# First eight score tiles read keys where they were loaded, token tiles 2 and 3 transposed by DMA, and a new order table

## The chip, the cores and the metric

The kernel runs on one core of a Trainium2 chip. The metric is the device time of one execution in microseconds (us), as the median of several runs. Engines are named as the profile names them: PE (TensorE matmul), PEld (TensorE weight load), DVE (VectorE), ACT (ScalarE), POOL (GpSimd), SP (SyncE, which issues all transfers here).

## What is computed

Attention over 4 batches, 8 heads, 768 positions, head size 64, in which each query sees the keys less than 16 positions away and, of every block of 32 keys, one summary (the maximum of the keys, the mean of the values). Its output, laid out as 3072 tokens of 512, goes through a layer norm and a two-layer network with a residual:

```python
k_sum = k.reshape(B, H, nb, block, D).max(axis=3)
v_sum = v.reshape(B, H, nb, block, D).mean(axis=3)
scores_l = scale * np.matmul(q, k.transpose(0, 1, 3, 2))      # kept where |i - j| < 16
scores_s = scale * np.einsum('bhsd,bhnd->bhsn', q, k_sum) + np.log(block)
a = softmax(concatenate([masked scores_l, scores_s]))
x = np.matmul(a, concatenate([v, v_sum]))                      # heads side by side: tokens x 512
xn = (x - mu) / np.sqrt(var + 1e-06) * g_ln
out = x + np.maximum(xn @ w_ch1, 0.0) @ w_ch2                  # 512 -> 2048 -> 512
```

Attention inputs are float32; the two weight matrices arrive as float64.

## The kernel before

**Tiles.** There are 24 token tiles T of 128 tokens and 48 score tiles t = 2T + hh, each for four heads. Batch 0 is score tiles 0 to 11 (`NEARLY`), which go the early way, in float32: `early_k`, `early_qk`, `softmax`, `early_transp`, `early_pv`. The others go by 16-bit pairs (`load_q`, `load_k`, `qk`, `transp`, `pv`). Two score tiles make a token tile; `ln` norms it and `lnT` transposes it into the 16-bit pair `xs`, two token tiles to a pair g. `lnT` does this on PE for T below `PET` (four 128x128 transposes into `tx`, then a copy on ACT and a subtraction on DVE), and for later tiles by a copy and a subtraction into `x16` and one DMA transpose of it.

**Keys of batch 0.** `fetch_k0` loads the keys of each head pair hp into the tile `k0[hp]`, the two heads of a pair on the two halves of the partitions (0 to 63, 64 to 127). `batch_k(0, hp)` takes the block maxima into `ksum` (printed `kmax`). `early_k` then copies, for one score tile, its window of keys and the 24 maxima side by side into `kx`: two copies on ACT, three on POOL. `early_qk` makes four float32 matmuls of 184 or 192 columns out of it, two variants v by the two halves pr.

**Network.** `fetch_w` loads 512 KB of float64 weights, `dec_w` takes them apart on DVE with a square on ACT for the scale, `conv_w` makes 16-bit pairs `wp` (high on ACT, low on DVE). `g1` makes hidden tiles `h` (12 matmuls to a half), `g2` the sums `a`. Later pairs use a Strassen scheme (`sp1`, `sp2`, `sw2`).

**Order.** Every step is recorded, not issued. `ORDER` gives the order in which steps are recorded, which sets who gets a tile's buffer first; `BANKS` gives each PSUM tile its bank; `RANKS` gives each instruction a priority. `Plan.schedule` is a list scheduler with costs for every operation: on each engine it takes the ready instruction with the lowest rank, and `Plan.issue` writes the instructions in the order of these planned starts. Each engine runs its own list in order. Where the plan has a gap on PE in the first tiles, `issue` repeats the `spare` transpose as a filler.

Of the kernel before, what the change touches and what calls it, by code (L numbers as in the profile page):

```python
# [39 lines left out]
PET = 4  # L40
# [20 lines left out]
    "&=&D&E%e%s%v%w%x&$&%%y%z&'%{&&%}&#%|&(&*&)&+$Y&.&/&>&X&`&]&V&W&Y&b&f&a&c&k&l&t&C&d&e&g&Z&[&^&_&h&z&m&n&o&p&r'<"
    "&u&v&q&w&x&y&{'>&?&@&B&J&R&H&P&N&L&F&G&I&K&M'E&s'B'='?'G'@'P'F'H'I'R&|'K'Y'Q'S(#(,()(%(-(2($('(+&}'A'C'D'V'T'U"
    "(('[&T'u'Z']'w(&'J'L'^(3'W'X'{'_(6(*(0&O&Q&S&U'v'x'y'z'|(8&i&j'#':'2'6','.'8'0'4'M'N'O'`(7(9(/(B(C'a'b(<'c(:(;"
    "(=(A(D(L'}(>(G(P(E(F(H'-'/'1'3(J(K(M(N(O(Q(.'5'7'9';(I(R(S'd'i'k'm's'q'g'e'f'h'o'j'l'n'p'r't(?(@'$'%'&'''(')'*"
    "'+(T(Z(1(4(5(_(U(](^(`(a(b(d(q(f(g(h(V(c(e(w(i(j(k(s(m(W(l(r(t(|(u(v(x(y)4(n)%(o(p(z({(})#)$)&)')()))0)/).)1)9"
    ")2)3)7)8):);)<)>)D)C(X(Y([)B)E)5)6)H)F)G)I)J)a)=)?)@)Q)A)M)K)L)N)O)])P)R)S)})Z)w)[)^)y)_)`)x)z){)|)*)+),)-*()b"
    ")c*-*'*)***2*+*,*.*/)T)U)V)W)X)Y*1*#*$*6*%*&)d)j)m)h)n)p)s)o)t)l)f)r)q)u*=*<)k)g)e*0*3*4*5*7*8*9*:)i)v*G*;*H*F"
    "*I*J*Z*Q*P*L*O*R*]*S*T*V*K*M*N*a*d*U*W*j*[*^*_*`*b*c*y*f*e*g*h*i*k*s*u*|*@*A*t*v+#*w*x*z*{*}+$+.+%+&*>*?+,*X*Y"
    "*B*C*l+'*m*n*D*E+-+/+0+1+3+D+6+5*o*p+7+8+F+(+9+:+)+;+<+M+2+4+=+>+S*q*r+E+G+O+H+I+K+N+P+Q+R+T+b+Y+*+++?+@+J+L+U"
    "+V+W+h+_+X+Z+[+]+^+`+a+A+B+C+c+d+e+f+g+i+j+k+l+m+n+o+p"  # L70
)
BANKS = (
    "12530273542251030314674216774060434256124251601472762136360451327560463215645471030640110237575136624013707045"
    "32146345212504317031760552660743271231726517467633246515277642500121313460310361345270764326502055016666372467"
    "1073547435543201211012061232150306721475261765430136455052417156033547751464572670105161023450"
)
RANKS = (
    "#X#F#&#>$@#0#$#2#6#'#:#?#W#4#8#%#(#*#/#,#+#C#Y#L#V#S#=#R#Z#B#^#[%p#3#k$7$<#{$,#<#j#A$-$1$4$9$=#g&=%N#.#P##$}%,"
    "#9%:%h%l%d#x$Y$N#y#}$+$2#1#7#;#@#I#D#K#E#)#M#Q$5#J$;$?$E$I#5#`#d#N#a#f#O#T#]#h#q#l#v#s#t#w#z#|$%$.$#$)#p#o#m#r"
    "#n#c$K$X$b$j#U$W$c$k$x%&%*%0%5%?%>%7%<%8%;%@%L%Z%^#G#e#i#H#_#b#u$'$>$0$B$D%E%P$8$3$:$6$A%O%Y%e%r%y%|&+$&$*$$$/"  # L80
    "$($H$Q$U$d$`$]$i$f$r%c%i$s%g%o%v&'&/&8#-$F%%%-%D%s'2';'d%4%m'i(0&6'F'K't$C$G$L$T$a$h$l$n$t$z$u%'%/%R%a$p$J%6%="
    "%C%K$y%[%f%}&)$M$m%9%B%H$o$q$w${%F&&%`%{&*&9&D&H&K$Z$^$[$g$_&E&Q&S&[&`&c&f%1$P$S$O$V$R%J%S%V%]%_%n%k&$%x&5&?&M"
    "%t%W%u%T%U&@&P&^&k'$'@'B'D'>$e%A%I%M%b$v$|%+%2%j%q%w%z&%&-(N&C'=&e'3&3&|%)%3%.&#&>&B&I&L&Z&i&u&J&N&U&Y&r&x&{'G"
    "'L'V'S'X'W'R&,'q&1&.%$&4&w'C'N%G'I'Q'`'n&(&0&7&;&F&V&b&l&m'''0&G&X&]&j&o&y&}&a&d&s&v'#'+'('/'H'O'^'c'a'['f'r'u"
    "'v'|(*(.(6&_&R&W&O&T&g'%')'.'1'4':'P(%&q(5&n&p','-'7'<'A'J'T'_'e'j'l'm'h's'{(#('(-(1(9(?%#%('g'p'}(F(L(Y(d(}'6"
    "'E(&(a(y)8)J)M'Z'k($(+&<&h&t&z(,(J(R(W(T(f(p(O(M([(Z(m(s&A(3(<(D(G'8'5'w()(/(;&:'9)))2)9)='z(4(B(S'Y(=(I(X(E(q"
    ")():(8(P'M'U'o'x(V(](`(c(((j(r(v({)*)$).)A)a),)4)/)6)b)T)5)@)>)I)<)C(x)')3)G*')O*-)m*;+1)|*^'y(H(K(U(t)?(|)#)%"
    ")&'?(_(e)K)N)7)U)Z)d)g)q)^)w)h*5*Q*B*V)F*H*N*S*X*Z*Y*[)-)_)f)j)l)e){*$*)*.(b(l(i(g(n(o)Q)n)V)p)S)W)Y)[*c*g*`*w"
    "+F+I,%,+,4,1,.,C)L)r)u)z)}'*(^(w)0)E);)i)k)o)s*%*(*+*/*3*7,7*9*=*<*?*A*F*>*C*e*l*z*}*r+?+J+^(Q(k(u)B)])`(z)P)R"
    ")c*0*2)1)x*#*&***@*I*O*R*T*],;*_*d*b*h*j*o*n*q+,+9+@+x*y+3+;+o)H*1*8*k*t)X)t)v)D*,*4*a*p*D+)+6+:+=+N+X+b,&*L*W"  # L90
    "*f+H(>(7(@(2(:+'+-+0+2+5+L+P+O+W+V+]+g+l+},),@,I,V,T,X,W*6*J*P+a+|,$,',*,-,3,8,F,M,S,0,=*K*{+&+++/*m+8+<+C+G,J"
    "*i+A+D+K+S+i+t,#,]*s+d+k+w+z,Y,h,w,{--,}-$-8->-B-G-K-],6,Q,^,z)y*:*E*U*x+$+#+%+*+.+4+j+Y+_+T*v+R+Z+`+e,(,,,2,5"
# [1547 lines left out]
```

## Time and profile before

| what | value |
|---|---|
| median of 3 runs | 602.65 us (601.69 to 604.08) |
| the profiled execution | 602.32 us, its span 600.5 us |
| PE busy | 585.4 us (97% of the span) |
| DVE busy | 527.8 us (88%) |
| ACT busy | 425.4 us (71%) |
| POOL busy | 195.5 us (33%) |
| granted TensorE clock, mean | 0.999 |

The span is the time from the first to the last instruction of the profiled execution; 1.8 us of that execution's time lie around it. Busy time of PE includes the fillers and the warm-up transposes. "Idle" below is the span or stretch less the busy time of that engine.

### The profile page before, as it was taken

To read this page: it belongs to the slowest core of one execution; us is meant where nothing else is said; L and a number is where in the kernel's file an instruction comes from. 1 tells how busy PE (TensorE), PEld (TensorE's weight loads), DVE (VectorE), ACT (ScalarE), POOL (GpSimd) and SP (SyncE) were. 2 spreads that over 40 slices of the span, in tenths; PEclk is the share of its full clock that TensorE was granted. 3 is DMA by queue.
4 is the path that set the end of the run, shared out by engine and by line. 5 is a ranking of instruction groups with operands and counts; after the bars stand their busy time and mean duration, and the time that the engine had idled before them with its cause. 6 is when DMAs were issued, how large, how long until landed. Compare 5 with 4: busy or idle time off the path is not lost. (4 is left out here: it accounts for less than half of the span.)

```text
span 600.5 us, 16320 instructions
## 1 busy us (share of the span) xinstructions
PE 585.4 (97%) x6055; PEld 444.0 (74%) x6055; DVE 527.8 (88%) x1351; ACT 425.4 (71%) x968; POOL 195.5 (33%) x355
## 2 busy tenths in 40 slices
PE   7989999999999999999999989999999999999997
PEld 6579846864975885786686776777687886987876
DVE  5999999999899999989979978799999989678465
ACT  4899967798886889478968586577688655473241
POOL 5121400044557554724333323226444310230000
PEclk9999999999999999999999999999999999999999
DMA  8995485528968968677986894657456653412300
GB/s 312 340 332 171 148 259 159 178 66 224 234 161 206 227 183 180 159 170 193 213 206 125 186 197 116 126 156 174 101 128 149 101 155 70 102 29 46 80 2 35
DMA packets 138175, 96.07 MB, mean 160 GB/s; under 512 B 96112, under 2 KB 120944, under 8 KB 138096
## 3 DMA queue, kind: packets, MB, share of 16 engines
q1 hardware_dynamic: 138096, 95.04, 62.9%
q8 instruction: 47, 0.77, 0.6%
q14 instruction: 32, 0.26, 0.1%
HBM read 66.27 MB, written 6.29 MB: 121 GB/s over the span
## 5 line engine op out<-in xcount | busy, mean ns | idle before, releaser
L563 PE MATMUL a<-wp,hh 128*128 128x512 f16 x640 | 190.4, 379 | 0.0
L563 PEld LDWEIGHTS <-wp 128*128 128x128 f16 x1968 | 152.3, 98 | 17.5 <-DMA xs<-x 0.8
L563 PE MATMUL a<-wp,hl 128*128 128x512 f16 x320 | 121.3, 379 | 0.0
L563 PEld LDWEIGHTS <-hh 128*128 128x128 f16 x736 | 68.8, 98 | 58.6
L563 PE MATMUL h<-xs,wp 128*128 128x256 f16 x960 | 109.5, 273 | 0.8 <-DMA xs<-x 0.7
L563 POOL TENSOR_TENSOR p<-p,p 128x512 f16<-128x512 f32 x72 | 74.0, 1039 | 101.8 <-ACT p L563 65.3
L563 ACT ACTIVATE p<-p,mn 128x184 f32<-128x184 f32 (+1 forms) x192 | 76.3, 441 | 12.2 <-DVE mn L563 11.9
L563 PEld LDWEIGHTS <-wd 128*128 128x128 f16 x1176 | 70.5, 98 | 9.8 <-issue 3.6
L563 PEld LDWEIGHTS <-hl 128*128 128x128 f16 x368 | 36.0, 98 | 38.9 <-DVE hl L563 0.6
L563 DVE CUSTOM_DVE_ANT_0 p<-s,mask,sv 128x184 f32<-128x184 f32 x144 | 52.8, 398 | 2.2 <-PE s L563 2.0
L563 ACT ACTIVATE in<-in 128x384 f32<-128x384 f32 (+2 forms) x66 | 39.2, 595 | 16.5 <-DVE kmax L563 5.4
L563 POOL COPY ksg<-ksum 128x48 f32<-128x48 f32 x48 | 20.9, 439 | 78.3 <-DMA ksg<-in_kt 62.9
L563 PE MATMUL qx<-xs,wp 128*128 128x128 f16 x672 | 43.4, 219 | 0.0
L563 ACT CAST p<-p 128x512 f16<-128x512 f32 x72 | 33.9, 507 | 1.0 <-DMA pT<-p 0.5
L563 DVE SCALAR_TENSOR_TENSOR x<-a,wsc,x 128x512 f32<-128x512 f32 x40 | 29.5, 740 | 2.7 <-PE a L563 2.6
L563 ACT ACTIVATE v<-vst,sv 128x512 f16<-128x512 f32 x36 | 25.8, 719 | 7.7 <-PE o L563 7.6
L563 ACT ACTIVATE xn<-x,mv,rs 128x512 f32<-128x512 f32 x20 | 16.3, 814 | 18.6 <-POOL mv L563 15.6
L563 ACT ACTIVATE hh<-h 128x512 f16<-128x512 f32 x40 | 23.9, 602 | 5.6 <-PE h L563 5.3
L563 DVE SCALAR_TENSOR_TENSOR qhl<-qs,sv,qhl 64x512 f16<-64x512 f32 x36 | 27.5, 765 | 0.1
L563 PEld LDWEIGHTS <-pT 128*128 128x128 f16 x720 | 25.6, 98 | 2.5
L563 DVE SCALAR_TENSOR_TENSOR v<-vst,sv,v 128x512 f16<-128x512 f32 x36 | 26.8, 745 | 0.7 <-ACT v L563 0.7
L563 PE MATMUL o<-v,pT 128*128 128x65 f16 (+1 forms) x720 | 27.2, 193 | 0.0
(257 smaller groups left out, 1277.7 us busy)
## 6 DMA issues: line engine op xcount, KB each, us to landing
raw<-in_w SPq DMA_DIRECT2D x32, 512.0 KB, 6.8
qs<-in_qt SPq DMA_DIRECT2D x72, 128.0 KB, 2.9
ksg<-in_kt SPq DMA_DIRECT2D x48, 184.0 KB, 2.9
out_x<-x SPq DMA_DIRECT2D x20, 256.0 KB, 2.9
in<-in_ks SPq DMA_DIRECT2D x24, 192.0 KB, 3.0
...
```

What stands on the lines that cost most here:

```text
L563: getattr(getattr(nc, self.ops[i].engine), op)(*a, **k)
```

## The change

`PET` goes from 4 to 2 and `DK = 8` is new. For the score tiles 0 to 7 `early_k` is not called, and `early_qk` reads the keys from `k0` and the maxima from `ksum` by separate matmuls into the same columns of the PSUM tile: two for v = 0 (160 and 24 columns), three for v = 1 (128, 32 and 32), where there was one each. `ksum` of batch 0 gets 32 columns for each head pair, cleared first, so that the third piece fills its columns. Score tiles 8 to 11 keep `kx`. Token tiles 2 and 3 take the `x16` way with a DMA transpose. The three tables are new throughout.

```diff
-PET = 4
+PET = 2
+DK = 8
...
 ORDER = (
-    "#)$Z#7#%$i#+#k#5#6#3#4$[#1#8$k#,$g$h#'$^###W#(#l#0#/#2#D$l#$$b$]$m#&#9#;#:#E#F#G#H#K#I#X$_$v#*#=#>#?#@#A#B#C#J"
+    "$b$T#+#&#9#($`#%#h#3#U$R#/#;$W#4###1#2#g$U$a#7$X#,#*#0$V#'#:#E$Z#=#>#?$]#$#F#G#H#J#@$S#5#6#A#B#C#)#<$8#8$e$c$d"
...
@@ batch_k
-            bt["m", b] = work("kmax" if b else "ksum", f"kmax{b}", [P, 4, NB], F32, 1 + (b == 0))
+            bt["m", b] = work("kmax" if b else "ksum", f"kmax{b}", [P, 4, NB if b else BLK], F32, 1 + (b == 0))
+            if b == 0:
+                nc.gpsimd.memset(bt["m", b][:], 0.0)
...
@@ early_qk
-                    q, k = qw[T][r].rearrange("p (h v l) -> p h v l", h=2, v=2)[:, hh], kx[t % 2][r]
-                    nc.tensor.matmul(ps[pr][:, v * NE : v * NE + w], q[:, v], k[:, v, :w], start=True, stop=True)
+                    q = qw[T][r].rearrange("p (h v l) -> p h v l", h=2, v=2)[:, hh]
+                    parts = [(0, kx[t % 2][r, v, :w])]
+                    if t < DK:
+                        s, m = k0[2 * hh + v][r, P * T : P * T + P + BLK], bt["m", 0][r, 2 * hh + v]
+                        parts = [(D, s[:, :P]), (0, s[:, P:]), (BLK, m)] if v else [(0, s), (P + BLK, m[:, :NB])]
+                    for at, k in parts:
+                        at += v * NE
+                        nc.tensor.matmul(ps[pr][:, at : at + k.shape[1]], q[:, v], k, start=True, stop=True)
...
@@ attend
         if t < NEARLY:
-            early_k(t)
+            if t >= DK:
+                early_k(t)
             early_qk(t)
```

What the new tables do to the order, at three places.

**The first score tile on PE.** Names ahead of the arrow are PSUM tiles (`s_0`, `s_1` the two halves pr); `kx`, `k_0`, `k_1`, `kmax` are the keys, `qw` the queries. Before:

```order
L563 MATMUL s_0_121<-kx,qw_94 128x184
L563 MATMUL s_1_122<-kx,qw_94 128x184
L563 MATMUL s_0_121<-kx,qw_94 128x192
L563 MATMUL s_1_122<-kx,qw_94 128x192
L563 MATMUL spare<-ident 128x128
```

Now:

```order
L563 MATMUL s_0_119<-k_0_90,qw_94 128x160
L563 MATMUL s_0_119<-kmax_109,qw_94 128x24
L563 MATMUL s_1_120<-k_0_90,qw_94 128x160
L563 MATMUL s_1_120<-kmax_109,qw_94 128x24
L563 MATMUL s_0_119<-k_1_91,qw_94 128x128
L563 MATMUL s_0_119<-k_1_91,qw_94 128x32
L563 MATMUL s_0_119<-kmax_109,qw_94 128x32
L563 MATMUL s_1_120<-k_1_91,qw_94 128x128
L563 MATMUL s_1_120<-k_1_91,qw_94 128x32
L563 MATMUL s_1_120<-kmax_109,qw_94 128x32
```

Four matmuls that alternated between the halves are ten, of which two or three in a row are on the same half.

**PE in front of the first hidden tile `h`.** `pp` are transposes of probabilities, `o` attention outputs, `tx` token-tile transposes. Before:

```order
L563 MATMUL o_229<-tail,pT_0_226 128x2x65
L563 MATMUL o_229<-vw_101,pT_0_226 128x65 x2
L563 MATMUL o_229<-tail,pT_1_228 128x2x65
L563 MATMUL o_229<-vw_101,pT_1_228 128x65 x2
L563 MATMUL pp_0_240<-ident,p_89 128x128 x3
L563 LDWEIGHTS wp_165
L563 MATMUL h_257<-xs_219,wp_165 128x256
```

Now:

```order
L563 MATMUL pp_0_247<-ident,p_89 128x128 x3
L563 MATMUL pp_1_245<-ident,p_89 128x128 x3
L563 MATMUL o_249<-vst_77,pT_0_248 128x2x65
L563 MATMUL o_249<-vw_101,pT_0_248 128x65 x2
L563 MATMUL o_249<-vst_77,pT_1_246 128x2x65
L563 MATMUL o_249<-vw_101,pT_1_246 128x65 x2
L563 LDWEIGHTS wp_207
L563 MATMUL h_278<-xs_229,wp_207 128x256
```

The last `pp` and the last output tile of the first eight score tiles stand ahead of the first `h` now; before they came between the first `h` matmuls.

**SP at its start and around the new DMA transposes.** `k` are the keys, `raw` the weights. At the start, before:

```order
L563 DMA k_3_93<-in_ks 128x768
L563 DMA k_1_91<-in_ks 128x768
L563 DMA qw_94<-in_qe 128x512
L563 DMA k_0_90<-in_ks 128x768
L563 DMA k_2_92<-in_ks 128x768
```

Now, and further on the two transposes of token tiles 2 and 3 (`in_` are loads of batch 1 for its scales):

```order
L563 DMA k_0_90<-in_ks 128x768
L563 DMA k_1_91<-in_ks 128x768
L563 DMA qw_94<-in_qe 128x512
L563 DMA k_2_92<-in_ks 128x768
L563 DMA raw_111<-in_w 128x1024
L563 DMA k_3_93<-in_ks 128x768
...
L563 DMA in_2_281<-in_ks 128x384
L563 DMA_TRANSPOSE xs_243<-x_2_244 128x8x128
L563 DMA in_3_282<-in_ks 128x384
L563 DMA_TRANSPOSE xs_243<-x_3_255 128x8x128
```

The fourth load of keys stands behind 512 KB of weights, and the second transpose behind a load that needs a staging buffer.

## Rows read from the trace of the kernel before

**Rows 1.** Page, part 1: busy us of PE (share of span), instructions.
```profile
PE 585.4 (97%) x6055; PEld 444.0 (74%) x6055; DVE 527.8 (88%) x1351; ACT 425.4 (71%) x968; POOL 195.5 (33%) x355
```

**Rows 2.** Busy time by stretch; columns as the first line says.
```profile
core 0: us, PE busy (x) PEld busy (x) DVE busy (x) ACT busy (x) POOL busy (x), PEclk, DMA share, GB/s
0.00:48.27 48.27, 41.74 (x296) 33.06 (x297) 40.70 (x145) 38.60 (x105) 14.85 (x77) 1.00 0.98 318
48.27:500.00 451.73, 446.30 (x4570) 330.31 (x4567) 418.46 (x1062) 345.13 (x785) 170.43 (x261) 1.00 0.69 167
500.00:600.50 100.50, 97.31 (x1196) 80.64 (x1193) 68.62 (x146) 41.71 (x80) 10.27 (x17) 1.00 0.23 53
```

**Rows 3.** The same view, from the first softmax pass to the last split of xs.
```profile
0.00:10.00 10.00, 6.95 (x45) 6.72 (x45) 4.00 (x10) 2.43 (x5) 7.31 (x46) 1.00 0.80 274
10.46:47.82 37.36, 33.88 (x247) 25.76 (x246) 36.23 (x135) 35.69 (x98) 7.33 (x30) 1.00 1.03 330
```

**Rows 4.** Waits of PE: us in total, times, longest us.
```profile
PE qx L563 <- ACT one L563: 1.6, 3, 0.7
PE qx L563 <- ACT two L563: 1.0, 1, 1.0
PE h L563 <- DMA xs<-x: 0.7, 1, 0.7
```

**Rows 5.** Timeline of PE: start us, us, instruction, tiles, shape, count.
```profile
13.02 3.11 PE L560 MATMUL spare<-ident 128*128 128x128 f32 x27
...
28.65 0.39 PE L563 MATMUL o<-vst,pT 128*128 128x130 f32 x2
28.88 0.55 PE L563 MATMUL o<-vw,pT 128*128 128x65 f32 x4
29.27 0.50 PE L563 MATMUL pp<-ident,p 128*128 128x128 f32 x3
29.70 0.91 PE L563 MATMUL s<-kx,qw 64*128 64x184 f32 x8
30.54 0.33 PE L563 MATMUL o<-ident 128*128 128x128 f32 x1
...
48.27 1.47 PE L563 MATMUL h<-xs,wp 128*128 128x256 f16 x12
...
52.50 5.40 PE L563 MATMUL h<-xs,wp 128*128 128x256 f16 x48
57.74 0.60 PE L563 MATMUL tx<-ident,xn 128*128 128x128 f32 x4
58.27 0.91 PE L563 MATMUL s<-kx,qw 64*128 64x184 f32 x8
```

**Rows 6.** Timeline of DVE: key maxima, first softmax pass, weight work, last xs split.
```profile
8.12 1.91 DVE L563 TENSOR_REDUCE kmax<-k 128x24 f32<-128x768 f32 x2 [2.12 <-DMA k<-in_ks]
10.46 0.36 DVE L563 CUSTOM_DVE_ANT_0 p<-s,emask 128x192 f32<-128x192 f32 x1 [0.43 <-PE s L563]
11.55 0.42 DVE L563 TENSOR_SCALAR wf<-raw 128x512 uint32<-128x512 uint32 x1
12.01 0.69 DVE L563 SCALAR_TENSOR_TENSOR wf<-raw,wf 128x512 uint32<-128x512 uint32 x1
...
45.95 0.16 DVE L563 RECIPROCAL rc<-rc 128x4 f32<-128x4 f32 x1
...
47.13 0.69 DVE L563 TENSOR_TENSOR xs<-tx,xs 128x512 f16<-128x512 f32 x1
47.73 1.40 DVE L563 SCALAR_TENSOR_TENSOR wp<-raw,wsc,wp 128x512 f16<-128x512 f32 x2
```

**Rows 7.** Timeline of ACT: copies of keys into kx.
```profile
10.43 0.52 ACT L563 COPY kx<-k 128x128 f32<-128x128 f32 x2 [1.04 <-PE s L563]
```

**Rows 8.** DMA transposes into xs, issue to landing; loads of weights (KB, median us).
```profile
DMA to landing us min/median/max: 3.1/3.5/4.0
raw<-in_w SPq DMA_DIRECT2D x32, 512.0 KB, 6.8
```

More of the change, by code (lines that the diff above doesn't have):

```diff
@@ L61 @@
[L61 to L65, printed above, removed]
@@ new lines @@
+    "$o$n&$&*&+&)&,&(&-$^#D#I#K#L#M#N#O#P#Q#R#S$_#V#W#X#[#Y#Z#]$f$g$h$i$j$Y#^#_#`#a#b#c#d$/#-#i#j#k#n#l#m$q#.#z#{#}"
+    "${$[$p$r$u$s#y$##o#e%'$}%&#|$$#p#q#s$&$'$v#t#T#f%$#r$%%%#u#v#w#x$($+$@$)$*$,$-$.$x%#$0$1$2$3$6$k$m$l%8$t%:$z$y"
+    "&%%7%D%9&.&1&0&/&3&2&4$|%(%+%/%0%,%-%)%*%;%=%.%?%A%<%>%@%B%3%P$w%C$4$5$7$9$I$:$<$=$;$>$?&7%2%F%5%R%_%m%1%E%G%H"
+    "%I%J%K%N%O%`$A$B$C$D$G%6%S%4%Q%T%W%X%U%V%e%b%c%d%M%g%L%^%l%]%k$E$F$H%f%Y%h%Z%i%a$J$K$L$M$N$O$P&9$Q&5&=&<&&&'%["
+    "%j%n%o%p%x%w%q%r%y%z%u%v%s%t%|&#%{%}&6&P&T&N&^&O&Q&W&;&X&Y&Z&[&]&_&d&R&S&U&V&`&i&c&e&f&g&h&l'4&n&w&m&o&p&q'5'="
@@ new lines @@
+    "&8&:&D&B&J&F&@&L&H&>&?&A&C&E&j&k':'6'7'8'?'9';'<'N'>'@'Q'I&s'A'B'H&r&t'C&u'J'K'L'M'O'P'S's'D&a'R'T'U'V'o'm&G&I"
+    "&K&M&b&v'*'&'.','('2'$'%''')'+'v(%'z($'{'x(#'w'y(*'n'p'q'r't(0&x&y'|(.(/(1(:'E'F'G'W'}(;()(B('(9(<(=(>'X'Y(4'Z"
+    "(2(3(5&z&{&|&}'#'0'-'/'1'3(D(C(E(F(G'u(?(6(H(I(@(A(J(K'['a'e'g'k'_'i']'c'^'`'b'd(((+'f'h'j'l(7(8(L(R(&(,(O(N(-"
+    "(U(T(M(Z(V(W(X(^(_(d(`(a(b(Y([(](r(i(j(k(l(m(s(c(e(f(x(g(h(n(p(t(u(v(w(y)&(o(q(z),)/)5)()')))*)+)-)1)0)2)3)4)6"
+    ")<(P(Q(S).);):)=)>)?)A)C)D)@)B)X)R({(|)E)F)G)T)H)S)U)V)W)Y)q)p)7)8)I)J)K)u)L)9)M)[)a)`)e)b)f)k)h)l)g)^)j)o)r)s"
@@ L83 @@
[L83 to L92, printed above, removed]
@@ new lines @@
+    "#b$#%^#K#-#O#f$U$J$S$`&%#+#0#6#;#>#@#B#C#/#F#G#m#p#q#s#t#r#z#v#x#|#}$&$i#Q$8$<$p$u$y%(%3%B%%%6%@#?#g#`#d#h#i#o"
+    "#A#y$/$1$6$:#w#{$)$0$4$9$=$A%$%+%2%;$F$I$R$X#)$E${%)%&%b%p%1%i&(&]&d'N%x&N&X'Q'R'g%-$?$3%*%.%7%<%A#n$$$%$($*$'"
+    "$,$-$2$.%0%>$5%9%E%j%m%w%|&&&,&/&3%?$>$H$M$K$P$O$W$T$a%K%O$[%F%T%]%f%k%n$;$@$B$G$Q$V$Y$]$d$j$e$n$t%,%=$r$x$+$C"
+    "$Z$_$c$h$b$o$m%#$}%`%o%M%z&+&7&;&@&5&8$N%5%L%N%S%W%X%U%_%Y&)&6%v&4&>$f$k$q$w$s%{&-&.&0&:&E&L%H%P%[%e%:%/%8%D%I"
+    "%R%Z%a%c%l%q'C&*&Z%}&K%V%Q&S&B&T&Y&v&y&s&|&G&P&R&W&_%g&'&n'9&r&{'/'>&w'%'5'T&1&9&?&D&O&[%d%r&#&A&F&M&b&2&Q&V&e"
@@ new lines @@
+    "&i%t&C&f&I&U&c&l'$')'@'E'P'Y%s%y&=&J&a&m&u'0'*','-'K'w(&(+&^&k&p'('.'2'4'8'6'<'B'J'L'Z'^'c'f&h&j&o&q&z''&x&}&t"
+    "'#'&'+':'?'H'F'D'A'M'S'W'X'_'b'i'n&H']'e'j's#R#S#U#P#Z'h'o't'x'{(%'z((($(,(<$z%''a'l(#(6'O'y()(9(E(L(X(b&$&<(f"
+    "(l)().'G'['d(/'1'='I'U'V(4(8'k(K(O(Q(T(Y([(W(`(x))(@(F(V(|(2(;(G(p(=(Z(i(R)%)*(o)3)5)-)G)L)O)l)w)8)Y)^)c*&*+'`"
+    "'}(*(3(:(?(B(D';(H(M(P(S(n(U(_(m(y(r)+(g(s(d(v(^(h(a(j({(t)&)[(u(}),)d)r*3)k)q)1)D)6)K);)Q)?)`)U*-(c)0)7):)=&`"
+    "(J(N(e)$)p)v){*$*1*4*_*7*:*M('(7(1(5(0(.(>(C(A(I)y*'*O)E)A)I)C*L*a+%+c+h+j+o+m+k+u,6,C,J,L,h(q)4)9)<)@(z)M)P)V"
@@ new lines @@
+    ")Z)/)g)i*=*P(k)2)>)B)F)T)X)_)a)f)h+e)o)u)t)|)j)n)m)x*d*h*w+4*(*9*J*R*0*@*H*W'm'r'q'u'p*G*l*r*z+$*p*o*u*s+-+;)'"
+    ")H)R)])b(w)J)N)S)W)z*%*,*.*2*6*<*A*E*D*I*;*?*>*B+0+M+r+z+9+A+F+N*Z*q*{+>*S*y+,+8*#*]*b*g*k)s)#)e*)*8*T*Q*|+&+."
+    "+7+)+5+J+q,(,.,@,<,G,;*`*e*j*n*C*t*x+#+(*F+@+D+H+L+^+{,),0+E+S+_+W+g+U+[+]+a+l+|,'+w,$,+,5,9,B,A,F,D,[,d,k,o,t"
+    ",|+2'v,-,>)}*U*Y*X+6+=+C+?*^*i*c*f*/*N*V*m+++1*[*v*}+:+K+Q+O+R+P+T*K+<+B+G+I+Y+b+f+i*5+n+p+s+t+y+v,#+},*,I,s,="
+    ",1,/,?,4,E,i,R,X,z,N,S,T,p,H,O,P,V-F-Y-M-X-g-c-q-w-2,`-<-K-T-*-R-Z+X+x,%,,,3,7,:,8,Q,U,c,j,Z'|(],e,l&g'7'3,b,v"
```

123 lines of the change are left out of this document (56 added, 67 removed).

## The prediction

> **What bounds the kernel now.** First the busy times [rows 1]: PE works 585.4 us of 600.5, DVE 527.8, so the sum has to be made on PE, as work plus idle time. Then busy time by stretch [rows 2] says where PE's 15.1 us of idle lie: 6.5 before the first hidden tile `h` starts at 48.27 (48.27 less 41.74), 5.4 between there and 500 us, 3.2 at the end, where the last sums and stores run out. The granted clock is at its full 2.4 GHz level (1.00) in every stretch, so no term here is a clock term. The stretch from the first softmax pass to the last split of `xs` [rows 3] shows what sets the start of `h`: DVE is busy 36.23 of 37.36 us, ACT 35.69, PE only 33.88, of which 3.11 are fillers [rows 5]. So up to 48 us the vector engines lead and PE has room; after it PE is full, and what PE must do is what the time is.
>
> Times below are sums against the profiled span of 600.5; 1.8 us lie around it (602.3), and that execution stands 0.3 below the median of 602.65. About 0.5%, 3.0 us, can be told from no change: faster means below 599.6, slower above 605.7.
>
> **The change, part by part.** I write G for the start of the first `h`. What counts is how far G moves, less the PE work that moves ahead of it, less the work that goes.
>
> *Split score matmuls, on PE.* A float32 matmul is two passes over its columns. Two passes of 130 columns take from 28.65 to 28.88, 0.115 each, 0.885 ns a column; four of 65 take from 28.88 to 29.27, 0.098 each, well over their columns, so short passes have a floor of 0.098 [rows 5]. A score tile before has eight passes of 184 or 192 columns. In sequence they would be 8 x 188 x 0.885 = 1.33; the tile takes 0.84 (29.70 to 30.54). So the two halves of the array work beside each other: of the 0.67 that perfect overlap would save, 0.49 or 74% is saved. Now each half has 2 x (160 columns, 24, 128, 32, 32) = 2 x (0.142 + 0.098 + 0.113 + 0.098 + 0.098) = 1.10. With perfect overlap the tile takes 1.10, +0.26; with none 2.20, +1.36. The order rows show two or three matmuls in a row on one half where there was one, which is why the share may fall, but the nearest row is the score tile itself, and I take its 74%: 2.20 - 0.74 x 1.10 = 1.38, +0.54. For eight tiles that is **+4.3 us, bounds +2.1 and +10.8**.
>
> *Fillers and moved work, on PE.* Fifteen fillers instead of 27: 12 x 3.11 / 27 = -1.4. One more `pp` (29.27 to 29.70, 0.43) and two more half outputs `o` (28.65 to 29.27, 0.62 each) stand ahead of the first `h`: 1.7, which the rest no longer has to do. PE's work ahead of G is then 41.7 - 1.4 + 1.7 + 4.3 = 46.3, bounds 44.1 and 52.8.
>
> *Copies into `kx`.* Sixteen ACT copies at 0.26 [rows 7] go, 4.2 us, and 24 on POOL. I cost them at nothing: POOL is mostly idle, and ACT, just behind DVE, drops further behind it. Its gain counts only if DVE is not what G waits for.
>
> *DVE ahead of G.* Counting DVE's list up to the split that completes the first `xs`, the new order has three more `wp` splits, one long and one short `wf` pass, and three small ones ahead of it: 3 x 0.70 + 0.69 + 0.42 + 3 x 0.16 = 3.7, less some 0.08 by which each overlaps the next (47.13 + 0.69 against 47.73), 3.0 [rows 6]. The gaps before were 37.36 - 36.23 = 1.1 [rows 3]; I let half of them be filled, -0.55, bounds 0 and -1.1. The first softmax pass waits for all four key maxima, as they stand ahead of it in DVE's list; the first could start at 8.12 + 1.91 = 10.0 instead of 10.46, 0.4 sooner, but the fourth load of keys is behind 512 KB of weights now, 1.6 to 1.9 us at 274 to 330 GB/s [rows 3], so the pass could be 1.1 later. I take +0.3, near the middle. **G = 48.3 + 3.0 - 0.55 + 0.3 = 51.0, bounds 49.7 and 52.4.** PE's 46.3 fit in front of it with 4.7 idle, against 6.5 now. A dearer split would be hidden up to some 49 us of PE work, as about 2 us of PE's early idle (no keys yet) cannot be filled; a cheaper one gains nothing.
>
> *Token tiles 2 and 3.* Eight PE transposes go, 2 x 0.53 (57.74 to 58.27) = -1.1 [rows 5]. The copy on ACT and the subtraction on DVE stay, with other operands. SP gets two transposes, and PE a wait in their place. PE asks for them after eight halves of `h` at 1.31 (5.24 / 4 from 52.50 to 57.74), two score tiles at 0.84 and a `pp`: G + 12.6. On DVE the second subtraction comes after ten long passes at 0.61, six at 0.34, and seven small ones at 0.08 behind the last `xs` split, which ended 0.45 before G: G + 8.2. The trace's transposes of the same size land 3.1 to 4.0 later [rows 8], G + 11.3 to 12.2. So nothing is waited for, by 0.4 us; bounds 0 and the rival below.
>
> *The rest of the tables.* From G to 500 us PE idles 5.4 us in short waits [rows 2], 3.3 of them in the five of [rows 4], each for an instruction that stood late in ACT's or DVE's list or a transpose. Another order makes other waits; no row prices it. The nearest is the 5.4 itself: I keep it, bounds 1.4 and 10.8. The end of PE's list has the same steps: 3.2 stays.
>
> **Sum:** G moves +2.7; moved work -1.7; transposes -1.1; together 0.0. Span 600.5, time **602.3 us**. By the bounds of G alone it is 601.0 to 603.7.
>
> **The rivals.**
>
> *The later waits shrink.* The order is what decides them, and a quarter left (1.4) gives 602.3 - 4.0 = 598.3. For it: after G, PE is busy 98.8% and the five longest waits are for a handful of instructions that a table can put earlier. Against: DVE is at 418 of 452 us there, so what one instruction gains another loses. Chance 0.31.
>
> *The halves of the array do not overlap any more* (the slower side). If PE takes matmuls strictly in order, three in a row on one half let the other stand. Then the split costs 10.8, PE's work ahead of G is 52.8, and with 2.0 of early idle G is 54.8: 602.3 - 2.7 + 6.5 = 606.1. It decides from about +7 us in all, 0.9 a tile, where PE passes DVE. For it: the order rows. Against: the score tile's 74%. Chance 0.14.
>
> *The transposes land late.* If these two take as long as a weight load, 6.8 us [rows 8], because weights fill the transfers in this stretch (DMA share 0.98 before G), `h` waits until G + 15.0, 2.4 us: 604.7. PE's list has nothing else to do there. Against: 3.1 to 4.0 in the trace. Chance 0.06, still within the 0.5%.
>
> The Trainium skill, page "VectorE: DVE Perf Modes", sections "The three transpose paths" and "Rules for kernel authors", speaks against this part: a 128x128 transpose should stay on TensorE where PSUM will do (390 ns there, 1309 by DMA). By an estimate from it, eight blocks one after the other would take 10.5 us and the time would be 608.4. The rows disagree on both sides: 0.53 / 4 = 0.13 us a block on PE, 3.1 to 4.0 for all eight by DMA.
>
> *The new order makes twice the later waits* (10.8): 607.7. Chance 0.09. That the change does not do what it says is out: the order rows show the splits, the two transposes and the missing copies.
>
> **How the numbers follow.** Forecast 0.40, late transposes 0.06: within 0.5% together 0.46. Shrinking waits: faster 0.31. No overlap 0.14 and doubled waits 0.09: slower 0.23. The likeliest time is 602.3. The range goes down past 598.3 to 597.5, which adds the lower bound of G to part of that case, and up past 606.1 to 606.5; left out are the doubled waits and the far ends of the others. Cases on both sides hold much of the chance, so the forecast's own range is 600.5 to 604.7.
>
> **What would show it.** Right: score tiles 0 to 7 at about 1.4 us each on PE, the first `h` at 50 to 52 us, PE idle ahead of it near 4.7, no wait for DMA at the first `h` of token tiles 2 and 3, and some 5 us idle between there and 500. The slower rival would show score tiles near 2 us and no slack on PE before `h`. The forecast is wrong in its main step if G stays where it is, or if DVE has slack ahead of it.

## The result, and the profile after

| what | before | after |
|---|---|---|
| median | 601.69 us of 5 runs | 607.34 us of 5 runs (606.21 to 608.63) |
| ratio, 95% interval | | 1.0085 (1.0060 to 1.0109) |
| measured again on another chip | 602.84 us of 33 | 607.17 us; 1.0069 (1.0046 to 1.0092) |
| profiled execution, its span | 602.32, 600.5 us | 606.21, 604.4 us |
| start of the first `h` (G) | 48.27 us | 55.80 us |
| PE's work, PE's idle ahead of G | 41.74, 6.53 us | 50.61, 5.19 us |

The change makes the kernel slower, by 0.7 to 0.85%. The forecast was 602.3 us, no change; the time lies above its range.

The page's busy times, as in [rows 1]:

```profile
PE 591.4 (98%) x6131; PEld 450.6 (75%) x6131; DVE 529.0 (88%) x1351; ACT 422.4 (70%) x952; POOL 185.0 (31%) x332
```

Busy time by stretch after, columns as in [rows 2]; ahead of G, from 10 to 20 us, and behind G:

```profile
core 0: us, PE busy (x) PEld busy (x) DVE busy (x) ACT busy (x) POOL busy (x), PEclk, DMA share, GB/s
0.00:55.80 55.80, 50.61 (x395) 42.22 (x395) 44.53 (x154) 40.94 (x107) 10.79 (x54) 0.97 0.94 306
10.00:20.00 10.00, 9.13 (x71) 7.51 (x69) 9.60 (x30) 6.70 (x18) 0.41 (x2) 0.83 1.08 358
55.80:500.00 444.20, 440.04 (x4555) 327.25 (x4555) 413.34 (x1047) 337.94 (x763) 164.53 (x261) 1.00 0.70 167
500.00:604.40 104.40, 100.78 (x1186) 81.13 (x1184) 71.13 (x151) 43.47 (x85) 9.71 (x17) 1.00 0.23 52
```

From G to the end the kernel takes 548.6 us, against 552.2 before [rows 2]. Of these 3.6 us PE's work gives 2.8 (543.61 before, 540.82 now) and its idle time 0.8. So in this execution the loss lies ahead of G and nowhere else: G moved by 7.53 us, PE's work ahead of it by 8.87, its idle time by -1.34. The granted clock is no longer at full level everywhere: its mean is 0.83 between 10 and 20 us.

Timeline of PE after (start us, us, instruction, tiles, shape, count, and in brackets the idle time ahead and what ended it). First the transposes at 12 to 16 us, then the score tile that answers to the one in [rows 5], then the way to the first `h`, then the first `h` that reads token tiles 2 and 3:

```profile
12.10 1.99 PE L563 MATMUL pp<-ident,p 128*128 128x128 f32 x6
13.88 1.49 PE L560 MATMUL spare<-ident 128*128 128x128 f32 x6
15.16 0.79 PE L563 MATMUL pp<-ident,p 128*128 128x128 f32 x3
15.79 0.49 PE L560 MATMUL spare<-ident 128*128 128x128 f32 x3
...
31.38 0.55 PE L563 MATMUL s<-k,qw 64*128 64x160 f32 x4
31.75 0.31 PE L563 MATMUL s<-kmax,qw 64*128 64x24 f32 x4
31.89 0.68 PE L563 MATMUL s<-k,qw 64*128 64x128 f32 x5
32.34 0.27 PE L563 MATMUL s<-kmax,qw 64*128 64x32 f32 x1
32.41 0.27 PE L563 MATMUL s<-k,qw 64*128 64x128 f32 x1
32.45 0.27 PE L563 MATMUL s<-kmax,qw 64*128 64x32 f32 x1
32.53 0.30 PE L563 MATMUL s<-k,qw 64*128 64x32 f32 x2
32.67 0.38 PE L563 MATMUL s<-kmax,qw 64*128 64x32 f32 x2
32.98 0.33 PE L563 MATMUL o<-ident 128*128 128x128 f32 x1
...
49.47 0.55 PE L563 MATMUL pp<-ident,p 128*128 128x128 f32 x3 [0.87 <-ACT pT L563]
...
51.28 0.49 PE L563 MATMUL o<-tail,pT 128*128 128x130 f32 x2 [0.65 <-ACT pT L563]
...
55.80 8.02 PE L563 MATMUL h<-xs,wp 128*128 128x256 f16 x72
...
68.16 0.55 PE L563 MATMUL pp<-ident,p 128*128 128x128 f32 x3
68.55 1.48 PE L563 MATMUL h<-xs,wp 128*128 128x256 f16 x12
```

Four readings. The score tile runs from 31.38 to 32.98, 1.60 us, where it took 0.84. Its first part, two matmuls in a row on each half (160 and 24 columns), ends after 0.51. Its second part, three in a row, takes 1.09: at 31.89 five passes of `k` stand together, the four of one half's two pieces and only one of the other half's. The transposes `pp` at 12.10 take 1.78 for six, against 0.43 for three in [rows 5], and six fillers take 1.28, against 0.69 (3.11 / 27 each): that is the lower clock. Ahead of G, PE waits for ACT's `pT` at 49.47 and 51.28, 1.5 us in all. And the `h` that reads token tiles 2 and 3, at 68.55, waits for nothing, 12.75 us behind G.

Timeline of ACT after, around these waits, and of SP, where the loads of `in` and of `raw` are issued, and the second of the two DMA transposes:

```profile
47.84 0.63 ACT L563 ACTIVATE in<-in 128x512 f32<-128x512 f32 x1 [0.46 <-DMA in<-in_qa]
...
48.47 0.56 ACT L563 CAST xs<-tx 128x512 f16<-128x512 f32 x1
48.93 0.48 ACT L563 COPY pT<-pp 128x384 f32<-128x384 f32 x1
50.14 0.63 ACT L563 ACTIVATE in<-in 128x512 f32<-128x512 f32 x1 [0.73 <-DMA in<-in_qa]
...
50.77 0.46 ACT L563 COPY pT<-pp 128x384 f32<-128x384 f32 x1
```

```profile
41.37 0.33 SPq L563 DMA_DIRECT2D raw<-in_w  x1
41.94 0.33 SPq L563 DMA_DIRECT2D in<-in_qa  x1
44.03 0.33 SPq L563 DMA_DIRECT2D raw<-in_w  x1
44.58 0.33 SPq L563 DMA_DIRECT2D in<-in_qa  x1
...
65.14 1.25 SPq L563 DMA_TRANSPOSE xs<-x  x1
```

ACT stands at 47.84 and 50.14 in front of passes over `in` (loads of batch 1 for its scales) whose data isn't there: 0.46 and 0.73 us of waiting, and 0.63 for each pass. Behind them in ACT's list are the cast of `xs` and the copies of `pT` for which PE waits. Both loads were issued right behind 512 KB of weights (41.37, 44.03). ACT's list ahead of G, by groups (busy us, mean ns, and idle time ahead):

```profile
L563 ACT COPY pT<-pp 128x384 f32<-128x384 f32 x16 | 7.7, 480 | 1.4 <-PE pp L563 1.1 <-PE o L563 0.3
...
L563 ACT ACTIVATE in<-in 128x512 f32<-128x512 f32 (+1 forms) x5 | 2.9, 586 | 1.2 <-DMA in<-in_qa 1.2
L563 ACT ACTIVATE x<-o,rc 128x64 f32<-128x64 f32 x9 | 2.1, 350 | 0.0
...
L563 ACT COPY kx<-k 128x158 f32<-128x158 f32 (+1 forms) x4 | 1.1, 309 | 4.1 <-DMA k<-in_ks 3.1 <-POOL kx L563 1.0
```

Before, 14 `pT` copies, 3 passes over `in` and no `x<-o` stood there (6.5, 1.7 and 0 us), and 16 copies into `kx` (4.4 us) where 4 are left. What the copies set free, the new order filled. DVE waits for the fourth load of keys ahead of its first softmax pass, at 11.17, and for ACT at the last `xs` split and just ahead of it:

```profile
10.30 0.95 DVE L563 TENSOR_REDUCE kmax<-k 128x24 f32<-128x768 f32 x1 [1.25 <-DMA k<-in_ks]
11.17 0.34 DVE L563 CUSTOM_DVE_ANT_0 p<-s,msk 128x184 f32<-128x184 f32 x1
...
53.82 0.16 DVE L563 TENSOR_SCALAR rc<-o 128x4 f32<-128x4 f32 x1 [0.46 <-ACT x L563]
54.68 0.69 DVE L563 TENSOR_TENSOR xs<-tx,xs 128x512 f16<-128x512 f32 x1 [0.69 <-ACT xs L563]
```

From that first pass to the end of that split DVE works 40.23 us of 44.20 and idles 3.97, where it had worked 36.23 of 37.36 and idled 1.13 [rows 3]. Of the 3.97 us it waits 1.15 for ACT (0.46 and 0.69), and longer for PE; the two largest of those waits, in us, times and longest:

```profile
11.17:55.37 44.20, 40.93 (x319) 33.11 (x320) 40.23 (x144) 38.09 (x100) 3.15 (x7) 0.96 0.99 320
```

```profile
DVE rc L563 <- PE o L563: 1.0, 2, 0.6
DVE p L563 <- PE pp L563: 0.6, 1, 0.6
```

### The profile page after: what moved, and what is told of

The parts are those of the page before. It is cut to its first block, busy times and chain, and to the rows that moved or that the text cites. A ratio compares the mean times of both kernels' runs of the same rounds, so it can differ in the third digit from the quotient of the medians.

```text
span 604.4 us, 16427 instructions
## 1 busy us (share of the span) xinstructions
PE 591.4 (98%) x6131; PEld 450.6 (75%) x6131; DVE 529.0 (88%) x1351; ACT 422.4 (70%) x952; POOL 185.0 (31%) x332
## 5 line engine op out<-in xcount | busy, mean ns | idle before, releaser
L563 POOL TENSOR_TENSOR p<-p,p 128x512 f16<-128x512 f32 x72 | 76.3, 1072 | 113.9 <-ACT p L563 81.3
L563 ACT ACTIVATE p<-p,mn 128x184 f32<-128x184 f32 (+1 forms) x192 | 76.3, 439 | 12.6 <-DVE mn L563 12.2
L563 ACT ACTIVATE in<-in 96x512 f32<-96x512 f32 (+2 forms) x66 | 38.8, 590 | 15.6 <-DVE mv L563 4.4
L563 POOL COPY ksg<-ksum 128x48 f32<-128x48 f32 x48 | 15.9, 333 | 55.7 <-DMA ksg<-in_kt 52.7
L563 ACT ACTIVATE qhl<-qs,sv 128x512 f16<-128x512 f32 x36 | 25.7, 714 | 7.1 <-PE s L563 6.8
L563 POOL TENSOR_SCALAR rs<-mv 128x1 f32<-128x1 f32 x24 | 9.0, 375 | 67.2 <-DVE mv L563 56.5
L563 DVE SCALAR_TENSOR_TENSOR v<-vst,sv,v 128x512 f16<-128x512 f32 x36 | 28.8, 801 | 0.1
L563 DVE SCALAR_TENSOR_TENSOR hl<-h,hh 128x512 f16<-128x512 f32 x40 | 26.9, 678 | 1.8 <-ACT hh L563 1.6
```

Source lines behind the costliest of these rows:

```text
L563: getattr(getattr(nc, self.ops[i].engine), op)(*a, **k)
```

## The experiments

The idea after the result: two causes that hide each other, the score tile's ten matmuls on PE (theory A) and the new order, in which ACT's list with its late loads sets G (theory C); beside them the granted clock (theory D). Theory B, in the first run alone, is that ten short matmuls are slow whatever their order. "The halves" are those of the array, pr = 0 and 1. The variants move single instructions within the two kernels; the orders are otherwise those of the kernel they start from.

| label | ratio to before, 95% interval | G us | PE work ahead of G | clock 10 to 20 us |
|---|---|---|---|---|
| (before) | 1 | 48.27 | 41.74 | 1.00 |
| (after) | 1.0085 (1.0060 to 1.0109) | 55.80 | 50.61 | 0.83 |
| after_again | 1.0069 (1.0046 to 1.0092) | 55.55 | 51.00 | 0.66 |
| e1_alternate | 1.0086 (1.0059 to 1.0114) | 56.06 | 49.71 | 0.83 |
| alternate_again | 1.0075 (1.0049 to 1.0101) | 53.65 | 48.37 | 0.83 |
| e2_new_order_copies | 1.0109 (1.0080 to 1.0139) | 55.08 | 44.91 | 1.00 |
| e3_old_order_split | 1.0055 (1.0030 to 1.0080) | 52.18 | 48.72 | 0.83 |
| e4_more_early_work | 1.0077 (1.0053 to 1.0101) | 55.13 | 49.79 | 1.00 |
| e5_in_passes_late | 1.0120 (1.0086 to 1.0154) | 54.36 | 50.84 | 0.66 |
| e6_alternate_in_late | 1.0093 (1.0062 to 1.0123) | 51.77 | 47.15 | 1.00 |
| e7_both_more_work | 1.0121 (1.0090 to 1.0152) | 51.73 | 47.84 | 1.00 |
| e8_old_order_alternate | 1.0013 (0.9991 to 1.0035) | 50.87 | 46.52 | 0.83 |
| e9_alternate_loads_first | 1.0022 (1.0003 to 1.0041) | 53.32 | 47.66 | 1.00 |
| e10_in_chain_late | 1.0089 (1.0057 to 1.0122) | 52.36 | 48.38 | 0.83 |
| e11_old_alternate_more | 1.0079 (1.0050 to 1.0108) | 53.48 | 50.10 | 1.00 |
| e12_loads_first | 1.0039 (1.0020 to 1.0058) | 53.63 | 49.41 | 1.00 |
| e13_alternate_three_loads | 1.0051 (1.0029 to 1.0073) | 52.42 | 46.48 | 1.00 |

G, work and clock are those of one profiled execution each; the ratios rest on 5 to 12 runs of a variant, so small differences are read from the ratios. How far one execution's G can be trusted shows in the two kernels that were profiled twice: 55.80 and 55.55 for the changed kernel, 56.06 and 53.65 for the halves in turn.

**The halves in turn.** In `early_qk`, for score tiles 0 to 7:

```diff
+                todo = []
...
-                    for at, k in parts:
-                        at += v * NE
-                        nc.tensor.matmul(ps[pr][:, at : at + k.shape[1]], q[:, v], k, start=True, stop=True)
+                    todo.append([(ps[pr], at + v * NE, q[:, v], k) for at, k in parts])
+                for pair in zip(*todo):
+                    for o, at, qv, k in pair:
+                        nc.tensor.matmul(o[:, at : at + k.shape[1]], qv, k, start=True, stop=True)
```

> The changed kernel with one edit: in score tiles 0 to 7 the matmuls of the two array halves are issued in turn (first half, second half, first half, ...) instead of two or three in a row on one half. Theory A (the split costs because matmuls in a row on one half hold the other half back): the three-piece part shortens, a score tile goes from 1.60 us to 1.1 to 1.3, PE's work ahead of the first h falls by 2.5 to 4 us, the first h moves from 55.8 to about 52.5, the time by -2 to -3.5 us (604 to 605.5). Theory B (the score tile is long because ten short matmuls have ten floors, whatever their order): score tiles stay within 0.1 of 1.60 and the time within 1 us of the changed kernel. Theory C (the loss is that of the new order's waits): score tiles shorten, but the first h stays later than 55 and the time within 1 us.

The same score tile on PE's timeline:

```profile
30.49 0.54 PE L563 MATMUL s<-k,qw 64*128 64x160 f32 x4
30.86 0.30 PE L563 MATMUL s<-kmax,qw 64*128 64x24 f32 x4
31.00 0.61 PE L563 MATMUL s<-k,qw 64*128 64x128 f32 x8
31.45 0.39 PE L563 MATMUL s<-kmax,qw 64*128 64x32 f32 x4
31.77 0.33 PE L563 MATMUL o<-ident 128*128 128x128 f32 x1
```

It takes 1.28 us (30.49 to 31.77), so B, that ten floors make the length whatever the order, is out. The first part is unchanged (0.51), the second takes 0.77 instead of 1.09. So A's mechanism is there, but the time isn't: the ratio stays at 1.0086, and a second time, later, at 1.0075:

> The changed kernel with alternating score tiles alone, as in the first run (1.0086, first h 56.1), beside the others on the same chip: Theory C says 1.006 to 1.009 again, the first h at 54 to 56; if it comes out level with the loads-first version (1.002), the loads were not what gained.

In the new order 2.6 us less of PE's work (8 x 0.32) bought nothing that the ratios show. Why G differs by 2.4 us between the two executions of this kernel is seen on PE. In the first it waits 1.51 and 0.55 us for ACT's `pT`, at 48.22 and 49.94, and then the granted clock falls: its mean is 0.57 from 50 to 54 us, where 0.5 is the lower level, 1.2 GHz:

```profile
50.00:54.00 4.00, 4.00 (x22) 3.94 (x22) 2.29 (x7) 2.52 (x10) 0.00 (x0) 0.57 0.56 196
```

The 22 passes from 49.94 take 4.24 us there. In the second execution the waits are 0.80 and 0.59 us, the clock stays at full level, and the same passes take 2.60. So part of what the shorter tiles save can be lost again behind a wait for ACT. That something other than PE's work holds G in this order is the next question.

**The split and the order apart.** First the new order with the old score tiles: the copies into `kx` are back, each about 1.5 us of plan time ahead of its tile, and four matmuls read them. Score tiles 8 and 9 find other keys in `kx` here, as their own copies, made at 6.3 us, are overwritten.

> The changed kernel's order with the old way of score tiles 0 to 7: their keys are copied into kx again (two copies on ACT, three on POOL for each) and four matmuls read it; everything else stands as in the changed kernel. Theory A (the split's extra 0.76 us a tile on PE is the main loss): PE's work ahead of the first h falls by 5 to 6 us; the first h comes 3.5 to 6 us sooner (50 to 52.3), the time is 601 to 604. Theory C (the new order's waits are the loss: late key loads, late loads for ACT): the first h stays at 54 or later, PE's idle ahead of it rises from 5.2 to over 9, the time stays within 1.5 us of the changed kernel.

PE's work ahead of G falls by 5.7 us and its idle time rises from 5.2 to 10.2, as C had it: G stays at 55.08, and the ratio is higher still. The run is not clean, since ACT has 4.1 us of copies to do again, but it shows that G can be as late with PE idle for 10.2 us ahead of it. Then the old order with the new score tiles, without copies:

> The kernel before with the split alone: score tiles 0 to 7 read k0 and ksum by ten matmuls, no copies into kx; the order is that of the kernel before. Theory A: score tiles take 1.6 us as in the changed kernel, PE's work ahead of the first h rises by 6; 6.5 us are idle there, of which about 2 cannot be used, so that the first h moves from 48.3 to 50 to 53 and the time goes up by 2 to 5 us (604 to 607). Theory C: the early idle takes most of the split, the first h stays below 49.5 and the time rises by less than 1.5 us (below 604).

```profile
0.00:52.18 52.18, 48.72 (x392) 42.20 (x393) 41.06 (x145) 35.55 (x89) 10.66 (x54) 0.97 0.91 295
```

Here PE's work rose by 7.0 us, 3.1 of that went into idle time, and G moved by 3.9, inside A's span; the ratio 1.0055 is 3.3 us. In the old order PE does set G once the score tiles are this dear. With the halves in turn:

> The kernel before with the split alone, its matmuls alternating between the halves. Split in a row in the old order gave a first h at 52.2 (48.3 without) and a ratio of 1.0055. Theory A (there PE's work sets the first h): score tiles take 1.35 instead of 1.60 us, PE's work ahead of the first h falls by 2 to 2.6, the first h comes at 49.5 to 50.7, the ratio to the kernel before falls to 1.000 to 1.004. Otherwise the first h stays at 51.5 or later and the ratio above 1.004.

G comes at 50.87, 0.2 us later than A said, and the ratio is 1.0013, which can't be told from none. A holds in the old order in both runs: the split costs 0.55% with three matmuls in a row and 0.13% in turn. Not all of the difference need be PE's order, since the runs with three in a row also had the lower clock: a mean of 0.995, against 0.998 in turn and 0.998 for the kernel before.

**The clock.** In front of score tiles 0 and 1:

```diff
+MORE = 8
...
+            if self.names[self.ops[i].stage] in [("early_qk", (0,)), ("early_qk", (1,))]:
+                op, a, k = self.ops[i].calls[0]
+                for _ in range(MORE):
+                    nc.tensor.transpose(*a, **k)
```

> The changed kernel with eight more 128x128 transposes of ident (into a region that is not read) ahead of each of the score tiles 0 and 1 on PE, where PE waits for loads anyway. Theory D (about 1.8 us of the loss are from TensorE's granted clock falling to its lower level, 1.2 GHz, between 12 and 15.5 us, because PE did less before): the granted clock of 10 to 20 us rises from 0.83 to 0.95 or more, the six-transpose pp that took 1.78 us takes under 1.0, the first h comes 1 to 1.8 us sooner, the time is 605 to 606.5. Theory not D: the clock row or the first h does not change, the time stays within 0.5 us or rises by up to 1.5, what the added transposes take (16 at 0.115).

```profile
55.13:500.00 444.87, 439.16 (x4538) 326.18 (x4538) 412.42 (x1046) 337.96 (x762) 164.19 (x260) 1.00 0.69 167
```

The granted clock from 10 to 20 us is at its full level, G is 0.67 us sooner, and the ratio, 1.0077, doesn't move. PE's idle time between G and 500 us is 5.71 instead of 4.16, which says little, as the repeat of the changed kernel has 5.43. In the old order the same transposes made it worse:

> The kernel before with the split alone, alternating (ratio 1.0013, granted clock 0.80 and 0.86 at 10 to 15 and 15 to 20 us), and eight more transposes of ident ahead of each of the score tiles 0 and 1. Theory D: the granted clock there returns to 1.00, the first h comes 0.5 to 1.5 us sooner, and the ratio is 0.998 to 1.001, so that the split alone is at no loss. Otherwise: ratio 1.001 to 1.004.

The clock at 10 to 20 us was 1.00, but score tile 0 starts only at 9.37 us behind the added work (8.68 without it), the clock fell between 30 and 40 us instead (0.61 and 0.70 in its two halves), and the ratio is 1.0079, outside both branches.

Neither run is clean, as the added work delays the score tiles behind it (tile 1 starts at 10.97 us in the first of the two, at 9.66 in the changed kernel). The mean clock that each run carries settles it without added work. On the chip on which the changed kernel was measured again, 15 of the 33 runs of the kernel before and 5 of the 11 of the changed kernel have a mean clock of 0.999 or more. They take 602.0 and 606.5 us on average, 4.4 us apart; over all runs the averages are 4.1 apart. So D is out as the main cause. The clock does go with the time of a run, though: the four runs of the kernel before with a mean of 0.994 take 604.7 us, and the two of the changed kernel with 0.991 and 0.992 take 609.1.

**ACT's passes moved.** The two passes over `in` are issued behind the first `h`; all other engines keep their order:

```diff
+LATE = 600
...
+        for c in (3, 4):
+            at[pos["batch_q", (1, c)]] = after_h + LATE
```

> The changed kernel with one move on ACT: the two passes over in (loads of batch 1 for its scales) that stood among the last pT copies before the first h, each late by its load, stand behind the first h. Nothing else moves. Theory C (in the new order it is the chain through ACT that sets the first h, not PE's work): the waits of ACT for in (1.2 us in the changed kernel) and the passes (1.6) go from in front of the pT copies, PE's waits for pT of 0.9 and 0.7 us shrink, the first h moves from 55.8 to 53 to 54.5, the time falls by 1 to 2.5 us. Theory A (PE's work, score tiles of 1.60 us, sets it): the first h stays within 0.6 of 55.8 and the time within 1 us.

> The two edits together: score tiles alternate between the halves, and the two in passes on ACT stand behind the first h. Theory C with A (either bound alone hides the other's gain, as alternating alone moved the first h by +0.3 only): the first h at 52 to 53.5, the time 2 to 4 us below the changed kernel. If the first h stays above 54.5, a third bound is there.

> The two edits and eight more transposes of ident ahead of each of the score tiles 0 and 1. If the granted clock of 10 to 20 us returns to 1.00 as it did with these transposes alone, the first h comes 0.5 to 1.5 us sooner than without them (51 to 53) and the time is 0.5 to 2 us lower; if the added work only takes its place on PE (16 at 0.085), it is the same or up to 1 us slower.

In the second of these G comes at 51.77 us, 4 us sooner, as C with A said, and yet the ratio is 1.0093 (1.0120 and 1.0121 for the other two). PE's and ACT's timelines show where it went:

```profile
51.77 8.02 PE L569 MATMUL h<-xs,wp 128*128 128x256 f16 x72
...
67.23 0.55 PE L569 MATMUL pp<-ident,p 128*128 128x128 f32 x3 [3.03 <-ACT p L569]
```

```profile
52.49 0.67 ACT L569 ACTIVATE in<-in 128x512 f32<-128x512 f32 x1
...
58.71 0.63 ACT L569 ACTIVATE in<-in 128x512 f32<-128x512 f32 x1 [2.24 <-DMA in<-in_qa]
```

PE waits 3.03 us at 67.23 for a softmax on ACT, which had waited 2.24 us at 58.71 for the next load of `in`. That load uses the buffer that the moved passes held: SP issues it at 53.27 instead of 48.59. The gain was given back 15 us behind G, and the clock added to it: behind the wait, from 68 to 72 us, it is 0.57, and the next 12 `h` matmuls take 2.54 us, 1.32 in the changed kernel's profile. The third's question stays open, as the clock from 10 to 20 us was 1.00 in the second already. Moving the whole chain (all passes and loads of that stretch, and the DMA transposes ahead of the loads) only moved the wait again:

> The changed kernel with alternating score tiles, the two loads first on SP, and all of the in passes of that stretch moved out of the way: in_12 and in_11 behind the first h on ACT, in_8 and in_9 behind the casts of token tiles 2 and 3, in_13 behind the softmax of score tiles 8 and 9, and the loads that use their buffers behind the two DMA transposes on SP. Theory C: the first h at 51.5 to 52.5 as when only two were moved, and the wait of 3.0 us at 64 to 67 us that took the gain back there is gone or under 1 us; the time is 2.5 to 4 us below the changed kernel (ratio 0.999 to 1.004). If the wait stays or one of the same size appears later, the new order's cost is not in these passes but in its ACT list as a whole, and the ratio stays at 1.007 or more.

The wait at 64 to 67 us is down to 0.76, but PE waits 2.50 us for a `pT` at 101 us, its idle time from G to 500 us is 9.16 us, and the ratio is 1.0089. The expectation's second branch came true. Its conclusion, that the cost is not in these passes but in ACT's list as a whole, isn't shown by this: passes can't be moved without moving what depends on them. The next runs leave the passes and move only their loads.

**The loads first.** Each load of `in` is issued one place earlier on SP, ahead of the 512 KB; nothing else moves:

```diff
-DMA raw_110<-in_w 128x1024
-DMA in_12_143<-in_qa 128x512
-DMA raw_123<-in_w 128x1024
-DMA in_11_141<-in_qa 128x512
+DMA in_12_143<-in_qa 128x512
+DMA raw_110<-in_w 128x1024
+DMA in_11_141<-in_qa 128x512
+DMA raw_123<-in_w 128x1024
```

> The changed kernel with alternating score tiles (as the first run) and, on SP, the two loads of in each issued ahead of the 512 KB weight load behind which they stood; nothing moves on the other engines. Theory C (ACT's chain sets the first h; of its delay 1.2 to 1.7 us are waits for these loads, 1.6 the passes): the waits for in go, the first h moves from 56.1 to 54 to 55 (passes moved away altogether gave 51.8), nothing is given back at 65 to 70 us, and the time is 1 to 2 us below alternating alone (ratio 1.005 to 1.007). If the loads land no sooner, nothing changes (1.0086).

> The changed kernel with the two loads of in issued ahead of the 512 KB weight loads on SP, and nothing else: score tiles keep three matmuls in a row. Theory C (ACT's chain sets the first h and the score tiles hide behind it): the first h at 53.5 to 54.5 instead of 55.8, ratio 1.003 to 1.006. Theory A (with ACT's waits gone PE's 50 us of work are the bound, as in the old order): the first h stays at 54.5 to 55.8, ratio 1.006 to 1.009, and only both edits together gain.

ACT's two passes in the version with the loads first alone:

```profile
46.48 0.63 ACT L569 ACTIVATE in<-in 128x512 f32<-128x512 f32 x1
...
47.94 0.65 ACT L569 ACTIVATE in<-in 128x512 f32<-128x512 f32 x1
```

No wait stands ahead of them any more, G is at 53.63, as C had it, and the ratio is 1.0039 where the changed kernel, on the same chip, has 1.0069: 2.1 us of median, 1.6 of mean, with a 95% interval of 0.4 to 2.8. Not all of G's 2.2 us are the loads'. The `pT` copy just ahead of the two passes starts at 46.10 against 46.90, so 0.8 us stood before them, in an execution whose clock was full from 10 to 20 us; the other 1.4 arise behind them. DVE's waits for ACT at the last `xs` split are gone too. The runs' mean clock is 0.997 in both kernels, so the gain in the ratio isn't the clock's.

With the halves in turn as well the ratio is 1.0022, more than C expected, against 1.0086 and 1.0075 for the halves in turn alone, on other chips. The profile shows less: ACT still waits 0.52 us for the second of the two loads, and G, 53.32, is near the 53.65 of the halves in turn alone. So the place of two loads on SP is worth 0.3% on one chip, and 0.5 to 0.6% by the comparison across chips. Whether turning the halves adds to it (1.0022 against 1.0039) lies inside the intervals. The last variant puts the fourth key load first too:

> The changed kernel with alternating score tiles, the two loads of in first, and the fourth load of keys, k_3, issued ahead of the first 512 KB of weights. If the late k_3 (landing at 10.30 instead of about 10.0) moves the whole chain of softmax passes, the first h comes 0.3 to 1 us sooner than 53.3 and the ratio is 0.999 to 1.002; if the first weights, now later, hold DVE up instead, nothing changes or it gets slower (1.002 to 1.005).

The first softmax pass on DVE comes at 10.39 instead of 11.52, and G is 0.9 us sooner (52.42), as expected. Yet the ratio, 1.0051, is not better: PE's idle time from G to 500 us is 6.36 instead of 4.39. Against the halves in turn alone on the same chip, 1.0075, the difference is inside the intervals, so this run does not confirm the gain of the loads by itself. The repeat of the changed kernel, for the chips' sake:

> The changed kernel itself once more, beside the others on the same chip: ratio 1.006 to 1.011 as at first, first h at 55 to 56.5. If it lies below 1.005 here, the differences between runs on different chips cannot carry the attribution.

No variant beats the kernel before; the nearest is the old order with the split in turn (1.0013).

## Why the prediction was wrong

**The step that failed** is "G = 48.3 + 3.0 - 0.55 + 0.3 = 51.0". It took DVE's list for what the first `h` waits for, with half of its gaps filled, and so hid a dearer split on PE behind it, and took ACT, which "drops further behind it", to cost nothing. Measured, in the same terms: DVE's first softmax pass came 0.7 later (10.46 to 11.17, forecast +0.3), its work up to the last `xs` split grew by 4.0 (36.23 to 40.23, forecast +3.0), and its gaps grew by 2.8 (1.13 to 3.97) where they were to shrink by 0.55. Together these are the 7.5 us by which G moved. The gaps are the largest miss: DVE waits there for PE and for ACT, whose lists were taken to be hidden. With the loads first, in an execution at full clock, they are 1.96 us.

For PE the old order shows it by experiment: the split alone moves G by 3.9 us and costs 0.55%, with DVE's list unchanged. For ACT, whose list was not counted, 9 `x<-o`, 2 `pT` and 2 `in` passes moved ahead of G (2.1, 1.2 and 1.2 us), and the loads for two of the passes over `in` stand behind weights; putting those loads first gives back 0.3% on one chip, 0.5 to 0.6% across chips.

Point by point, against the terms of the sum:

- *Split, +4.3 us*: 8 x (1.60 - 0.84) = 6.1, inside the bounds 2.1 and 10.8. The reason for the size was right in kind: matmuls in a row on one half lose the overlap. In turn, the tile takes 1.28, 0.18 above the bound of 1.10. What the split costs in time is 0.55% in the old order, 0.13% in turn.
- *"A dearer split would be hidden up to some 49 us of PE work"*: 48.72 us of work moved G by 3.9 in the old order, with PE idle for 3.46, so only 3.1 of the 7.0 us were hidden. By the rule G would have been 48.72 + 2.0 = 50.7; it was 52.18, and the 2.0 us of idle time that were to be left are 3.5.
- *Fillers and moved work*: 15 fillers as read from the order; PE's work behind G fell by 2.8, the 1.7 and 1.1 of the text.
- *Copies at nothing*: not contradicted, but not shown by itself. In the old order they went together with the split, and G came later.
- *Token tiles 2 and 3*: right. The second transpose was issued at 65.14 (G + 9.3, where G + 8.2 was the figure), PE asked at G + 12.75 (12.6 was the figure), and nothing waited: 3.4 us from issue to use for eight blocks. The Trainium skill, page "VectorE: DVE Perf Modes", section "The three transpose paths", gives 1309 ns for one block by DMA; by an estimate from it, eight one after the other take 10.5 us. The trace disagrees here too.
- *Later waits kept, 5.4 and 3.2*: 4.16 and 3.62.
- *"No term here is a clock term"*: wrong. In the changed kernel's profile the pieces from 12.10 to 15.79 us cost 1.7 us more than at full level: six `pp` 1.78 against 2 x 0.43, six fillers 1.28 against 0.69, three `pp` 0.63 (15.16 to 15.79) against 0.43. It varies from execution to execution, and in other executions the clock falls elsewhere too.

The 8.87 us on PE ahead of G are then 6.1 for the split, 1.7 moved, 1.7 for the clock, less 1.4: 8.1; 0.8 is not accounted for. The rival that came nearest is "the halves do not overlap any more" (606.1, G 54.8): its time and its sign were right, and its place; its mechanism only in the three-matmul part. In the new order it is not the whole cause: with the old score tiles G was still at 55.08, though ACT had copies to do again there.

The causes hide each other. With matmuls in a row, the old order costs 0.55%, the new one 0.69 to 0.85%. In turn, the old order costs 0.13%, the new one 0.75 to 0.86%. With the loads first in the new order, 0.39% and 0.22%. The 0.2% that stays is about as much as the split in turn costs in the old order; that it is the same cost is not shown.

**Still open.** What turning the halves adds when the loads are first. What the passes over `in` themselves cost at their place (2 x 0.63 us on ACT), since moving them moved loads. The DMA transposes were not tried apart from the tables; that PE didn't wait for them rests on the trace alone. How much of the halves' gain in the new order was lost to the clock: the 17 runs with the halves in turn have a mean clock of 0.994, the 16 of the changed kernel 0.997.
